# Attention plus two MLPs in split fp32: the probabilities of three batches copied into one-pass tiles before their transposition

## Chip, cores and metric

The kernel runs on one core of one Trainium2 chip. The metric is device time in microseconds of one execution. Five engines work side by side: TensorE (PE, with its weight loads listed as PEld), VectorE (DVE), ScalarE (ACT), GpSimd (POOL) and SyncE (SP), which issues nearly all DMAs.

## What is computed

Four batches of 12 heads, 448 positions, 64 numbers per head; then two MLPs over the 1792 tokens. Inputs of the MLPs arrive as 64-bit floats, everything is computed to fp32 accuracy.

```
q_n, k_n = rmsnorm(q, g_q), rmsnorm(k, g_k)
scores = (q_n @ k_n.T) / sqrt(64);  attn = softmax(scores)
x = (attn @ v)                      # heads joined: 1792 x 768
x = relu(x @ w_in) ** 2 @ w_out     # 768 -> 2048 -> 768
out = ((x @ w1) * (x @ w2)) @ w3 @ w_out2   # 768 -> 1024 -> 768
```

## The kernel before

**Products in three passes.** PE multiplies one-pass fp32 operands (type `F32R`, `fp32r` in the rows). A number is split into a high and a low part of that type, and a product is high·high + high·low + low·high: three matmuls, lines 262 to 264 (`mm3`). `w3 @ w_out2` is multiplied out ahead of time (`gen_w3o`) and stored as `w3o`.

**Weights.** They come in units of 128x384 or 128x512 numbers. In the first MLP pass (batch 0) a unit is loaded as 64-bit words (SP, line 180), its halves are turned into two 32-bit pieces by ACT (line 194) and POOL (line 200), DVE joins them (line 207), and the fp32 unit is stored to DRAM (line 215). The three later batches load that fp32 copy (line 183). Every unit is then split: ACT copies the high part (line 106, `hl<-raw`), POOL or DVE subtracts for the low part (line 114). Four buffers for 64-bit units and four for fp32 ones are used in turn; a load waits for its buffer. `advance` (line 240 onwards) issues loads, pieces, joins and splits a fixed number of units ahead of the matmul that uses them.

**Attention.** The main loop runs over the 48 heads `h` and one more round. Each round has, for head `h`: scores in two halves (`stage_qk`, lines 524 and 525), the maximum on DVE (lines 526, 527), the exponential on ACT (`stage_exp`, line 542), which writes the probabilities `p`, 112 x 448 for each of four chunks. In the same round head `h - 1` is finished: `stage_t` transposes its probabilities on PE, 16 transpositions in four blocks (line 564; three blocks of 128 columns, the last of 64). The probabilities are the stationary operand, so each transposition is a weight load of 128 (or 64) columns and a matmul with the identity `ident`, 112 columns. ACT copies the transposed block as high part (`ptr`, `pte`), DVE subtracts for the low part, and `stage_v` multiplies with `v` (line 616). The normalised keys are transposed too (`stage_k`, line 508): they are split already, lie in `fp32r` tiles and use `ident_r`, an identity of that type.

**Filling.** Between the steps of a round, `fill(n)` puts matmuls of the MLP of the batch before into PE's queue: during heads 0 to 11 the product `w3o`, during heads 12 to 23 the MLP of batch 0 (with the 64-bit weights), during 24 to 35 that of batch 1, during 36 to 47 that of batch 2; that of batch 3 stands alone at the end. Every engine and SP's queue work in order; the order is set by a scheduler when the kernel is built.

**Buffers touched.** `p` has six tiles of 112 x 448 fp32, in pool `t3`; a tile is free again when its head's transpositions are done.

Of the kernel before, what the change touches and what calls it, by code (L numbers as in the profile page):

```python
# [8 lines left out]
F32 = mybir.dt.float32  # L9
F32R = mybir.dt.float32r  # L10
# [19 lines left out]
def attention_moe_kernel(  # L30
# [15 lines left out]
    nc = tc.nc  # L46
    B, P, H, C, D = q_nat.shape
    S = P * C
# [40 lines left out]
    t3 = ctx.enter_context(tc.tile_pool(name="t3", bufs=3))  # L89
# [9 lines left out]
    ident = const.tile([P, P], F32, name="ident")  # L99
    ident_r = const.tile([P, P], F32R, name="ident_r")  # L100
# [3 lines left out]
    def copy_on(eng, out, in_):  # L104
        if eng == "a":
            nc.scalar.activation(out=out, in_=in_, func=AF.Copy)  # L106
        elif eng == "g":
            nc.gpsimd.tensor_scalar(out=out, in0=in_, scalar1=1.0, scalar2=1.0, op0=ALU.mult, op1=ALU.mult)
        else:
            nc.vector.tensor_copy(out=out, in_=in_)  # L110
# [418 lines left out]
    def stage_exp(h, s):  # L529
        if not (0 <= h < NH):  # L530
            return
        d = heads[h]
        nb, o = d.pop("nb"), d.pop("sc")
        i = h % 2
        if s == 0 and i == 0:
            sums2[h // 2] = small.tile([P, 2, C], F32, name="sm", tag="sm")
        sm = sums2[h // 2]
        c0 = 2 * s
        for j in range(2):
            c = c0 + j  # L540
            p = d["p"][c] = t3.tile([P, S], F32, name="p", tag="p", bufs=6)
            nc.scalar.activation(  # L542
                out=p, in_=o[j], func=AF.Exp, scale=d["rq"][:, c:c + 1], bias=nb[:, j:j + 1],
                accum_out=sm[:, i, c:c + 1],
            )
        if s == 1 and i == 1:
            nc.vector.tensor_scalar(out=sm, in0=sm, scalar1=1e-9, scalar2=None, op0=ALU.add)
            rs = small.tile([P, 2, C], F32, name="rs", tag="rs")
            nc.vector.reciprocal(out=rs, in_=sm)
            wide = t1.tile([P, C, 2, D], F32, name="rsw", tag="rsw")  # L550
            nc.gpsimd.tensor_scalar(
                out=wide, in0=rs.rearrange("p i c -> p c i").unsqueeze(3).to_broadcast([P, C, 2, D]),
                scalar1=1.0, scalar2=1.0, op0=ALU.mult, op1=ALU.mult,
            )
            sums2[h // 2] = wide.rearrange("p c i d -> p c (i d)")

    def stage_t(h, kc):
        if not (0 <= h < NH):
            return
        d = heads[h]  # L560
        k0, kn = KCS[kc]
        ps = ps_pt.tile([128, 512], F32, name="pt", tag="pt")
        for c in range(C):
            nc.tensor.transpose(ps[:kn, c * P:(c + 1) * P], d["p"][c][:, k0:k0 + kn], ident)  # L564
        if kn == 128:
            t = t3.tile([128, 2, S], F32R, name="ptr", tag="ptr", bufs=3)
            hi, lo = t[:, 0, :], t[:, 1, :]
            d["pt"][kc] = [hi, lo]
        else:
            t = t1.tile([128, S], F32R, name="pte", tag="pte")  # L570
            hi, lo = t[:kn, :], t[kn:, :]
            d["pt"][kc] = [t]
        copy_on("a", hi, ps[:kn, :S])
        d["lo"].append((lo, ps[:kn, :S], hi.bitcast(F32)))
# [67 lines left out]
    def fill(n):  # L642
# [18 lines left out]
        out=gg, in0=g_sb[:, 0:1], scalar=float(D) ** -0.5, in1=g_sb[:, 1:2], op0=ALU.mult, op1=ALU.mult  # L661
# [8 lines left out]
    for h in range(NH + 1):  # L670
# [5 lines left out]
        stage_qk(h, 0)  # L676
        fill(n)
        stage_exp(h, 0)
        if h % H != 1:
            stage_x(h - 2)  # L680
        stage_t(h - 1, 0)
        stage_t(h - 1, 1)
        fill(n)
        stage_lo(h - 1)
        if h < NH:
            v_prep(h)
        fill(n)
        stage_k(h + 1)
        stage_t(h - 1, 2)
        stage_t(h - 1, 3)  # L690
        fill(n)
        stage_lo(h - 1)
        stage_qk(h, 1)
        fill(n)
        stage_exp(h, 1)
        fill(n)
        stage_v(h - 1)
# [64 lines left out]
```

## Time and profile before

| | us |
|---|---|
| median of 3 runs | 1253.63 (1252.76 to 1253.79) |
| span of the profiled execution, first to last instruction | 1246.1 |
| PE busy | 1173.5 (94%) |
| PE weight loads busy | 1060.8 (85%) |
| POOL, ACT, DVE busy | 780.3, 728.9, 708.0 |
| matmuls / DMA packets | 6192 / 102129 |

The profiled execution is given by its span; its own time is not listed apart, and the three runs lie 6.7 to 7.7 us above the span, for what comes ahead of the first instruction and after the last. A weight load runs beside a matmul, so PE and PEld add up to more than the span. The recorded end of a matmul is modelled; how fast they follow each other is read from their starts.

### The profile page before, as it was taken

How to read it: one execution, taken by the hardware profiler on the slowest of the kernel's cores; microseconds unless marked ns; L12 is line 12 of the kernel's file. 1: busy time of each engine (PE TensorE's matmuls, PEld its weight loads, DVE VectorE, ACT ScalarE, POOL GpSimd, SP SyncE). 2: the span in 40 equal slices, each digit the busy share in tenths (PEclk: the TensorE clock that was granted, in tenths of full speed). 3: DMA queues.
4: the chain of work that ended last, by engine and by line, in shares of the span. 5: the costliest groups of instructions: out<-in, count | busy, mean ns of one | idle time of the engine just before them, and what ended most of it. 6: DMA issues, size and time to landing. Idle time of an engine off the chain costs nothing.

```text
span 1246.1 us, 18719 instructions
## 1 busy us (share of the span) xinstructions
PE 1173.5 (94%) x6192; PEld 1060.8 (85%) x6192; DVE 708.0 (57%) x1314; ACT 728.9 (58%) x1553; POOL 780.3 (63%) x772
## 2 busy tenths in 40 slices
PE   3789999898889899999999999999999999999998
PEld 2678888887777788999999999999999999999998
DVE  6699888867887775547567555655664421012110
ACT  5788876756655655566645555656645554443342
POOL 6775435645675665675776664755766556678773
PEclk9999999899999999999999999999999999999999
DMA  7774446876766655344333344332333333433342
GB/s 218 237 225 137 150 140 183 267 215 217 236 205 212 207 158 159 106 117 113 113 102 114 96 130 128 105 105 85 112 95 88 92 114 107 113 108 108 103 121 94
DMA packets 102129, 178.71 MB, mean 143 GB/s; under 512 B 11056, under 2 KB 65552, under 8 KB 102032
## 3 DMA queue, kind: packets, MB, share of 16 engines
q1 hardware_dynamic: 98576, 172.01, 46.6%
q10 hardware_dynamic: 3456, 5.51, 1.2%
q8 instruction: 49, 0.80, 0.3%
q14 instruction: 48, 0.39, 0.1%
HBM read 149.95 MB, written 27.53 MB: 142 GB/s over the span
## 4 chain that ended last, share of the span: by engine, by line
PE 69%; DVE 10%; DMA 7%; ACT 5%; POOL 5%; issue 4%; SPq 0%; ACTq 0%; DVEq 0%; POOLq 0%
PE mm L263 18%; PE mm L262 18%; PE mm L264 18%; PE pt L564 4%; PE kv L616 4%; POOL hl L114 2%; PE sc L524 2%; DMA raw<-w_in 2%; PE sc L525 2%; DVE raw L207 2%; DVE nb L526 2%; ACT p L542 2%; DMA kn<-k_nat 1%; DMA raw<-w 1%; ACT hl L106 1%
## 5 line engine op out<-in xcount | busy, mean ns | idle before, releaser
L114 POOL TENSOR_TENSOR hl<-raw,hl 128x384 fp32r<-128x384 f32 (+1 forms) x383 | 444.6, 1164 | 254.1 <-ACT hl L106 251.2
L106 ACT ACTIVATE hl<-raw 128x384 fp32r<-128x384 f32 (+1 forms) x416 | 233.2, 564 | 149.2 <-PE mm L264 82.2
L263 PE MATMUL mm<-x,hl 128*128 128x448 f32 (+1 forms) x832 | 306.4, 368 | 9.4 <-POOL x L114 9.4
L262 PE MATMUL mm<-x,hl 128*128 128x448 f32 (+1 forms) x832 | 311.0, 374 | 4.0 <-ACT x L106 1.8
L264 PE MATMUL mm<-x,hl 128*128 128x448 f32 (+1 forms) x832 | 305.5, 367 | 0.9 <-POOL hl L114 0.9
L262 PE MATMUL mm<-act,hl 128*128 128x448 f32 (+1 forms) x640 | 238.6, 373 | 0.0
L263 PE MATMUL mm<-act,hl 128*128 128x448 f32 (+1 forms) x640 | 235.8, 368 | 2.2 <-POOL act L114 1.7
L264 PE MATMUL mm<-act,hl 128*128 128x448 f32 (+1 forms) x640 | 234.7, 367 | 1.4 <-POOL hl L114 1.0
L542 ACT ACTIVATE p<-sc,nb,rr 112x448 f32<-112x448 f32 x192 | 137.3, 719 | 75.4 <-DVE nb L527 74.8
L263 PEld LDWEIGHTS mm<-x,hl 128*128 128x128 f32 x832 | 158.2, 190 | 23.2 <-POOL x L114 11.1
L262 PEld LDWEIGHTS mm<-x,hl 128*128 128x128 f32 x832 | 158.1, 190 | 18.9 <-ACT x L106 2.9
L264 PEld LDWEIGHTS mm<-x,hl 128*128 128x128 f32 x832 | 158.2, 190 | 14.9 <-POOL hl L114 2.0
L200 POOL TENSOR_SCALAR raw<-raw 128x384 uint32<-128x384 uint16 (+1 forms) x110 | 87.7, 798 | 84.6 <-DMA raw<-w_in 35.3
L526 DVE TENSOR_REDUCE nb<-sc 112x1 f32<-112x448 f32 x192 | 113.2, 616 | 37.7 <-PE sc L525 36.7
L263 PEld LDWEIGHTS mm<-act,hl 128*128 128x128 f32 x640 | 122.0, 191 | 12.9 <-POOL act L114 3.0
L264 PEld LDWEIGHTS mm<-act,hl 128*128 128x128 f32 x640 | 122.0, 191 | 11.8 <-POOL hl L114 1.8
L262 PEld LDWEIGHTS mm<-act,hl 128*128 128x128 f32 x640 | 122.2, 191 | 9.4 <-ACT act L106 0.2
L114 DVE TENSOR_TENSOR ptr<-pt,ptr 128x448 fp32r<-128x448 f32 x144 | 86.9, 618 | 69.8 <-ACT ptr L106 69.2
L207 DVE SCALAR_TENSOR_TENSOR raw<-raw 128x384 uint32<-128x384 uint32 (+1 forms) x120 | 85.5, 715 | 51.6 <-POOL hl L114 43.5
L564 PE MATMUL pt<-ident,p 112*128 112x112 f32 (+1 forms) x768 | 99.4, 265 | 12.6 <-DVE ptr L114 9.7
L194 ACT ACTIVATE raw<-raw 128x384 f32<-128x384 f32 (+1 forms) x120 | 71.1, 599 | 68.1 <-DMA raw<-w 25.0
L114 POOL TENSOR_TENSOR act<-gf,act 128x448 fp32r<-128x448 f32 x80 | 96.9, 1212 | 8.1 <-ACT act L106 3.2
(80 smaller groups left out, 1542.7 us busy)
## 6 DMA issues: line engine op xcount, KB each, us to landing
raw<-f_in SPq DMA_DIRECT2D x96, 192.0 KB, 2.4
raw<-f_out SPq DMA_DIRECT2D x72, 256.0 KB, 2.6
raw<-f SPq DMA_DIRECT2D x96, 192.0 KB, 2.4
raw<-w_in SPq DMA_DIRECT2D x32, 384.0 KB, 3.5
raw<-w_out SPq DMA_DIRECT2D x24, 512.0 KB, 4.5
raw<-w SPq DMA_DIRECT2D x32, 384.0 KB, 4.0
raw<-w3o SPq DMA_DIRECT2D x48, 256.0 KB, 2.7
qt<-q_t SPq DMA_DIRECT2D x48, 224.0 KB, 2.8
```

What stands on the lines that cost most here:

```text
L106: nc.scalar.activation(out=out, in_=in_, func=AF.Copy)
L114: e.tensor_tensor(out=out, in0=in0, in1=in1, op=ALU.subtract)
L194: nc.scalar.activation(out=hi, in_=hi, func=AF.Prelu, scale=2.0**-112, alpha=-(2.0**32))
L200: nc.gpsimd.tensor_scalar(out=t[:, :n, 0], in0=low, scalar1=2.0**-13, scalar2=2.0**-14 - 0.5, op0=ALU.mult, op1=ALU.add)
L207: nc.vector.scalar_tensor_tensor(out=f[:, :n].bitcast(U32), in0=t[:, :n, 1], scalar=3, in1=t[:, :n, 0], op0=ALU.logical_shift_left, op1=AL ...
L262: nc.tensor.matmul(ps, w[:, 0, wk, :], x[0], start=(i == 0), stop=False)
L263: nc.tensor.matmul(ps, w[:, 0, wk, :], x[1], start=False, stop=False)
L264: nc.tensor.matmul(ps, w[:, 1, wk, :], x[0], start=False, stop=(i == last))
L526: nc.vector.tensor_reduce(out=nb[:, j:j + 1], in_=o[j], axis=AX.X, op=ALU.max, negate=True)
L542: nc.scalar.activation(out=p, in_=o[j], func=AF.Exp, scale=d["rq"][:, c:c + 1], bias=nb[:, j:j + 1], accum_out=sm[:, i, c:c + 1],)
L564: nc.tensor.transpose(ps[:kn, c * P:(c + 1) * P], d["p"][c][:, k0:k0 + kn], ident)
L616: nc.tensor.matmul(ps[:, :S], w, m, start=(n == 0), stop=(n == len(ops) - 1))
```

## The change

From head 12 on (`h >= H`), the two chunks of probabilities that one `stage_exp` makes are copied by a DMA on SP's queue from `p` to a new tile `pw` of type `F32R`, 112 x 896 words, bit for bit. The transpositions of those heads read `pw` and `ident_r` and write the PSUM tile as `F32R`. `p` becomes three tiles of two chunks each (as many bytes as before); `pw` has three more of that size. The region of SBUF that is kept for DMA descriptors made in software is set to 1 KB.

```
+        pp = t3.tile([P, 2, S], F32, name="p", tag="p")
         for j in range(2):
             c = c0 + j
-            p = d["p"][c] = t3.tile([P, S], F32, name="p", tag="p", bufs=6)
+            p = d["p"][c] = pp[:, j, :]
             nc.scalar.activation(
                 out=p, in_=o[j], func=AF.Exp, scale=d["rq"][:, c:c + 1], bias=nb[:, j:j + 1],
                 accum_out=sm[:, i, c:c + 1],
             )
+        if h >= H:
+            words = t3.tile([P, 2, S], F32R, name="pw", tag="pw")
+            nc.sync.dma_start(out=words.bitcast(F32), in_=pp)
+            d["p"][c0:c0 + 2] = [words[:, 0, :], words[:, 1, :]]
...
         ps = ps_pt.tile([128, 512], F32, name="pt", tag="pt")
+        to, one = (ps.bitcast(F32R), ident_r) if h >= H else (ps, ident)
         for c in range(C):
-            nc.tensor.transpose(ps[:kn, c * P:(c + 1) * P], d["p"][c][:, k0:k0 + kn], ident)
+            nc.tensor.transpose(to[:kn, c * P:(c + 1) * P], d["p"][c][:, k0:k0 + kn], one)
...
-    nc = bacc.Bacc("TRN2", target_bir_lowering=False, num_devices=1)
+    nc = bacc.Bacc("TRN2", target_bir_lowering=False, num_devices=1, dynamic_dma_scratch_size=1024)
```

How the order of the instructions moves, at three places. In the changed kernel the lines behind `stage_exp` have other numbers: the exponential is line 543, the copy 549, the transposition 570.

SP's queue, during the first MLP pass, around the copy of the first half of head 14. Before:

```order
L180 DMA raw_2735<-w_out 128x1024
L215 DMA f_in<-raw 128x384
L180 DMA raw_2783<-w_out 128x1024
L215 DMA f_in<-raw 128x384
L180 DMA raw_2802<-w_out 128x1024
L215 DMA f_out<-raw 128x512
L422 DMA v<-v_in 128x256
```

and now:

```order
L180 DMA raw_2716<-w_out 128x1024
L549 DMA pw<-p 112x896
L215 DMA f_in<-raw 128x384
L180 DMA raw_2764<-w_out 128x1024
L215 DMA f_in<-raw 128x384
L180 DMA raw_2783<-w_out 128x1024
L215 DMA f_out<-raw 128x512
```

The copy stands behind the 51st load of 64-bit weights (`raw_2735` before, `raw_2716` now); the 52nd and 53rd, and three stores, stand behind the copy.

ACT, around the exponentials of the second half of head 14. Before:

```order
L106 ACTIVATE hl<-raw 128x384
L194 ACTIVATE raw_2841<-raw_2841 128x512
L106 ACTIVATE hl<-raw 128x512
L194 ACTIVATE raw_2864<-raw_2864 128x512
L330 ACTIVATE r<-mm 128x448
L106 ACTIVATE hl<-raw 128x512
L333 ACTIVATE act<-r 128x448
L542 ACTIVATE p,sm<-sc,nb,rr 112x448 x2
```

and now:

```order
L106 ACTIVATE hl<-raw 128x384
L194 ACTIVATE raw_2764<-raw_2764 128x512
L106 ACTIVATE hl<-raw 128x512
L194 ACTIVATE raw_2783<-raw_2783 128x512
L330 ACTIVATE r<-mm 128x448
L106 ACTIVATE hl<-raw 128x512
L333 ACTIVATE act<-r 128x448
L543 ACTIVATE p,sm<-sc,nb,rr 112x448 x2
```

The rows read alike, but the weight units are others: ahead of these exponentials stood the units loaded 54th and 55th (`raw_2841`, `raw_2864`), now stand those loaded 52nd and 53rd (`raw_2764`, `raw_2783`). The turning of the 64-bit weights has moved back by two units against the attention there.

PE, at the first two blocks of transpositions of a head of batch 1. Before:

```order
L263 MATMUL mm<-x,hl 128x448
L264 MATMUL mm<-x,hl 128x448
L564 MATMUL pt<-ident,p 128x112 x8
L262 MATMUL mm<-x,hl 128x448
L263 MATMUL mm<-x,hl 128x448
```

and now:

```order
L263 MATMUL mm<-x,hl 128x448
L264 MATMUL mm<-x,hl 128x448
L570 MATMUL pt<-ident_r,pw 128x112 x8
L262 MATMUL mm<-x,hl 128x448
L263 MATMUL mm<-x,hl 128x448
```

PE's order stays as it was but for two exchanges of neighbours; the transpositions stand at the same place and read `pw`.

## Rows read from the trace of the kernel before

**Rows 1.** Windows: stretch, length, busy time of PE, PEld, DVE, ACT, POOL, clock, DMA.

```profile
192.00:498.00 306.00, 276.57 (x1416) 243.16 (x1415) 231.33 (x415) 191.69 (x414) 183.07 (x195) 0.97 0.68 206
498.00:768.00 270.00, 270.00 (x1466) 247.87 (x1465) 161.21 (x285) 156.21 (x341) 178.18 (x166) 1.00 0.39 113
768.00:1028.00 260.00, 260.00 (x1411) 238.62 (x1410) 134.08 (x244) 147.58 (x323) 162.11 (x148) 1.00 0.34 100
```

**Rows 2.** Waits of PE, 192 to 498 us: waited for, total us, times, longest.

```profile
PE sc L524 <- ACT p L542: 14.9, 13, 2.7
PE pt L564 <- DVE ptr L114: 9.2, 10, 3.4
```

**Rows 3.** Timeline of PE, 619.6 to 621.3 us: start, length, what (head 29).

```profile
620.07 0.93 PE L564 MATMUL pt<-ident,p 112*128 112x112 f32 x8
...
621.06 0.36 PE L263 MATMUL mm<-act,hl 128*128 128x448 f32 x1
621.26 0.37 PE L264 MATMUL mm<-act,hl 128*128 128x448 f32 x1
```

**Rows 4.** Timeline of PE, 114.8 to 116 us, a run of key transpositions.

```profile
115.00 0.34 PE L264 MATMUL mm<-x,hl 128*128 128x384 f32 x1
115.17 0.46 PE L508 MATMUL kv<-ident_r,khl 112*128 112x112 f32 x4
...
115.71 0.34 PE L263 MATMUL mm<-x,hl 128*128 128x384 f32 x1
```

**Rows 5.** Timeline of PEld near 626.5 us, in narrow windows.

```profile
626.43 0.23 PEld L508 LDWEIGHTS kv<-ident_r,khl 112*128 112x128 f32 x2
...
626.69 0.20 PEld L564 LDWEIGHTS pt<-ident,p 112*128 112x128 f32 x2
```

**Rows 6.** Groups by form, PEld, whole span: count, busy us, mean ns, idle.

```profile
L564 PEld LDWEIGHTS pt<-ident,p 112*128 112x128 f32 x576 | 63.0, 143 | 17.8 <-DVE ptr L114 9.9 <-issue 3.0 <-PE kv L508 0.3
...
L564 PEld LDWEIGHTS pt<-ident,p 112*64 112x64 f32 x192 | 19.1, 113 | 3.2 <-DVE ptr L114 2.0 <-PE pt L564 0.4
```

**Rows 7.** DMA issues, 192 to 498 us: count, KB each, median us to landing.

```profile
raw<-w SPq DMA_DIRECT2D x32, 384.0 KB, 4.0
...
kn<-k_nat SPq DMA_DIRECT2D x3, 448.0 KB, 4.2
```

**Rows 8.** DMA, 498 to 768 us: queue (packets, MB, share), one issue.

```profile
q1 hardware_dynamic: 18614, 28.80, 37.2%
...
kn<-k_nat SPq DMA_DIRECT2D x3, 448.0 KB, 3.8
```

**Rows 9.** Timelines of ACT and PE: last exponential and first transposition, heads 12, 18, 32.

```profile
192.08 0.19 ACT L542 ACTIVATION_READ_ACCUMULATOR p<-sc,nb,rr 112x1 f32 x1
...
194.58 0.93 PE L564 MATMUL pt<-ident,p 112*128 112x112 f32 x8
...
339.96 0.20 ACT L542 ACTIVATION_READ_ACCUMULATOR p<-sc,nb,rr 112x1 f32 x1
...
345.45 0.93 PE L564 MATMUL pt<-ident,p 112*128 112x112 f32 x8
...
681.53 0.19 ACT L542 ACTIVATION_READ_ACCUMULATOR p<-sc,nb,rr 112x1 f32 x1
...
687.20 0.93 PE L564 MATMUL pt<-ident,p 112*128 112x112 f32 x8
```

**Rows 10.** Waits of SP's queue, 498 to 768 us.

```profile
SPq L183 <- POOL hl L114: 190.8, 100, 5.3
```

**Rows 11.** Timelines near 220 us: SP's queue, and the first half of head 14.

```profile
218.20 0.33 SPq L180 DMA_DIRECT2D raw<-w_out  x1
...
222.78 0.20 ACT L542 ACTIVATION_READ_ACCUMULATOR p<-sc,nb,rr 112x1 f32 x1
```

**Rows 12.** Chain of waits, 192 to 498 us, shares of the stretch by line.

```profile
by line: issue 10.0%; POOL hl L114 8.9%; DMA raw<-w_in 7.5%; DVE raw L207 6.1%; DMA raw<-w 5.3%; ACT p L542 4.6%; DVE nb L526 4.2%; PE mm L262 3.6%; PE mm L264 3.5%; PE mm L263 3.4%; DMA raw<-w_out 3.1%; ACT hl L106 3.0%; DMA kn<-k_nat 2.9%
```

## Prediction

> **What bounds the kernel now.** I read the busy times by stretch first, then PE's waits, then single stretches of the timelines. The change touches heads 12 to 47, which fill three stretches: 192 to 498 us (heads 12 to 23, beside the first MLP pass with its 64-bit weights), 498 to 768 and 768 to 1028. In the second and third PE is busy for 270.0 of 270 and 260.0 of 260 us [rows 1]: PE alone sets their length, and a nanosecond taken from it is a nanosecond of the end. In the first it is busy for 276.6 of 306 us, so 29.4 us are idle, and the largest items are waits for the exponential on ACT (14.9 us, 13 times) and for the low parts of transposed blocks on DVE (9.2 us, 10 times) [rows 2]. There the chain of waits runs through the weights: DMA of w_in, w and w_out 7.5, 5.3 and 3.1%, POOL's splits 8.9%, DVE's joins 6.1% [rows 12]. So the change has a clear place to win in the last two stretches, and a stretch with no room to spare ahead of them.
>
> **What a transposition costs.** Eight fp32 transpositions start at 620.07; the second matmul behind them starts at 621.06, and the next 0.20 later [rows 3]. 0.99 less an ordinary 0.20 to 0.21 us leaves 785 ns, 98 ns for each. The new kind stands in the trace already, in the transpositions of keys: a one-pass fp32 tile of 112 partitions and 128 columns as weights, 112 columns of identity moving. A run of four of these starts at 115.17, the second matmul behind it at 115.71; less an ordinary 0.17, that is 0.37 us, 92 ns each [rows 4]. A longer run goes at the pace of its weight loads: from the second load of the four at 626.43 to the load behind the fourth at 626.69 there are three steps, 87 ns each [rows 5]. So the new kind isn't four times as fast, nor twice: the matmul gets shorter, and the weight load becomes the limit. For blocks of 128 columns I take 98 - 87 = 11 ns at most and 98 - 92 = 6 at least, 9 as the middle. For the blocks of 64 columns no one-pass row exists. A load of 64 columns takes 113 ns where one of 128 takes 143 [rows 6], so 30 less; 87 - 30 = 57 ns, and the gain is 98 - 57 = 41. Bounds are 6 ns (a load that costs as much as one of 128) and 98 - 50 = 48 (112 moving columns at the granted 2.4 GHz are 47 ns, and something for the start). A head has 12 of the one and 4 of the other: 12 x 9 + 4 x 41 = 272 ns, between 96 (16 x 6) and 324 (12 x 11 + 4 x 48). If loads of the new kind could follow as fast as the fp32 pair in the same group, whose second starts 61 ns after the first (0.20 - 0.14 from 626.69), it would be 16 x 37 = 592 ns; I take the keys' rows, which are of the same type and shape, and keep 592 for the far end.
>
> The Trainium skill (TensorE: Matmul & The Clock Gate, LDWEIGHTS) says that a weight load takes its columns divided by 1.2 GHz, which would be 107 ns for 128 columns and 53 for 64. By that rule the 128-column transpositions would get slower, and a head would gain only 12 x (98 - 107) + 4 x (98 - 53) = 72 ns. The trace has 87 and 61 ns where the rule has 107, so it speaks against the rule's size.
>
> In the last two stretches 24 heads gain 24 x 0.272 = **6.5 us**, all of it on PE. In the first stretch 12 heads gain 3.3 us of PE time; with a tenth of that stretch not PE's, and the waits beside it not shortened, I count half, **1.6 us**.
>
> **What the copies cost.** 72 copies of 112 x 896 words are added, 401 KB each (392 in the rows' KB). Size and partitions are nearest to the loads of k, 448 KB over 112 partitions: 4.2 us from issue to landing in the first stretch, weights of 384 KB take 4.0 there [rows 7], and 3.8 us in the second [rows 8]. Between SBUF and SBUF no row exists. I take 4.2 and 3.8, and 3.2 to 5.2 as bounds. Up to one other issue (0.33 us) [rows 11] stands ahead of a copy that is ready, so some 4.5 and 4.1 us from the last exponential to the transpositions. What time is there? For head 12 the last exponential ends at 192.27 and its transpositions start at 194.58: 2.3 us. For head 18 it is 340.16 to 345.45: 5.3 us [rows 9]. These are the least and the most of the twelve heads of the first stretch, which spread between them. Spread evenly, the mean shortfall against 4.5 is (4.5 - 2.3)² / (2 x 3.0) = 0.81 us, 9.7 us over 12 heads. PE would wait in a new place, but each such wait also lets ACT and DVE catch up, and the 24.1 us of waits of [rows 2] shrink by some of it. Between nothing and all I take half: **4.8 us**. With 3.2 + 0.3 it is half of 2.9 (1.4 us), with 5.2 + 0.3 all of 20 us.
>
> From head 24 on the least time between is that of head 32, 681.72 to 687.20, 5.5 us [rows 9]. 4.1 is under it. There SP waits 1.9 us at a time for a buffer (190.8 us in 100 waits, 5.3 the longest) [rows 10], and a copy can stand behind such a wait. What is left for head 32, 1.4 us, covers most of one; I count nothing, and name it below.
>
> The Trainium skill (DMA: Bandwidth & Descriptors, Anatomy of one DMA) gives a fixed 2.0 us plus bytes at 436 GB/s, which would be 2.9 us for a copy. By that the first stretch would lose 0.8 us in place of 4.8, and the sum would be 1246.3. The loads of k take 4.2 us here against 3.1 by the rule, so the trace disagrees.
>
> The rest costs nothing: the copies' traffic lies beside PE, DMA being busy for 0.39 and 0.34 of the later stretches [rows 1]; ACT and the three pairs of `p` keep their size; `p` comes free earlier, when copied; no DMA is issued by POOL, so the 1 KB is room alone.
>
> **The sum.** -6.5 - 1.6 + 4.8 = -3.3 us. The trace's span is 1246.1 us and the median of the runs 1253.6, 7.5 more for what lies around it, which the change doesn't touch. **1250.3 us** against 1253.6.
>
> **The rivals.**
>
> *Copies hold the weights up (slower).* SP's queue works in order, and a copy waits in it for its exponential. In the trace the 52nd load of 64-bit weights went out at 218.20, while the first half of head 14 was done at 222.98 [rows 11]; in the new order that load stands behind the copy, 4.8 us later. Behind it in the DMA rings it also waits for the copy's bytes: the queue needs 0.372 x 270 us for 28.8 MB [rows 8], so 1.4 us for 0.401 MB. For it: the first stretch's chain runs through weight loads, 15.9% of 306 us or 49 us, a dozen loads of 4 us [rows 12]. Against it: ACT's order has moved back by one or two weight units at those places, as the loads do. If half of the dozen are set back by 1.4 us, 8.4 us come on top: 1258.7; if all, and some of the wait with it, 1267. It decides once more than 3.3 us (two or three loads) are lost so.
>
> *Nothing gained at the loads (no change).* At the low bound, 24 x 0.096 = 2.3 us and 0.6 in the first stretch, less 4.8: 1255.5. For it: 92 ns in the one run of keys that is followed by plain matmuls [rows 4]. It is then slower by 0.15%. The rule of the Trainium skill on weight loads (above) belongs here: 72 ns a head, 1.7 + 0.4 - 4.8, 1256.3.
>
> *Loads at the fp32 pace.* 592 ns a head: -14.2 - 3.6 + 4.8, 1240.6. Against it stand the keys' rows of the same type.
>
> *Copies late in the last two stretches too.* One of 5.2 us behind a wait of 1.9 comes 1.6 us after head 32's 5.5; with 24 heads at half of that, 19 us more, 1269. For most heads there is more time than for head 32.
>
> *The type changes nothing.* If a transposition of the new type took 98 ns, only the waits would be left: 1253.6 + 4.8 = 1258.4. The keys' loads speak against it.
>
> **How the numbers follow.** 0.2% (2.5 us) is about what a measurement of this kernel can tell from no change. The forecast has 0.38 (own range 1246.5 to 1253, of which 0.05 within 0.2%); weights held up 0.27 (0.22 slower, 0.05 within); nothing gained 0.20 (0.16 within, 0.04 slower); loads at the fp32 pace 0.08; late copies 0.04; no effect of the type 0.03. Faster: 0.33 + 0.08 = 0.41; within: 0.05 + 0.05 + 0.16 = 0.26; slower: 0.22 + 0.04 + 0.04 + 0.03 = 0.33. The range 1241 to 1262 takes in the forecast with its bounds, nothing gained, and the milder part of weights held up; the far ends of the others are left out.
>
> **What would show it.** Transpositions of heads 12 on should follow at some 87 ns, those of 64 columns at 50 to 60; the stretch from head 24 to 47 should be 6 to 7 us shorter with PE still busy all through. Copies should land 3.5 to 4.5 us after their issue. In the first stretch PE should wait for `pw` by a few us in all, heads 12 and 13 first, and its waits for ACT's exponential should shrink. I am wrong if ACT or POOL wait much longer for weights there than now, if PE waits for `pw` after head 24, or if the blocks of 64 columns are no faster than the others.

## The result, and the profile after

The changed kernel takes **1239.49 us** (1239.34 to 1240.05, 4 runs) against 1253.2 us (1251.29 to 1253.79, 4 runs): ratio 0.9894, 95% interval 0.9878 to 0.9909. The forecast was 1250.3 with a range from 1241 to 1262, so the sign was right and the size was not: 13.7 us were gained, not 3.3. That the sign came out right is luck, as the fifth run below shows.

First the windows of the changed kernel, columns as in [rows 1].

```profile
192.00:498.00 306.00, 278.95 (x1451) 248.61 (x1450) 236.37 (x416) 193.84 (x419) 191.13 (x198) 0.97 0.77 243
498.00:768.00 270.00, 267.64 (x1461) 244.16 (x1460) 160.57 (x288) 156.19 (x340) 178.03 (x166) 1.00 0.51 148
768.00:1028.00 260.00, 260.00 (x1419) 237.60 (x1418) 134.20 (x244) 146.99 (x321) 163.98 (x148) 1.00 0.45 134
```

In the first stretch PE has 35 more matmuls done in the same 306 us than in [rows 1]; in the second it is idle for 2.4 us where it had no idle time. DMA is busier by 0.09 to 0.12, which is the copies (without them, in the sixth run below, DMA is at 0.69, 0.38 and 0.33). How long each part lasts is read from the first transposition of heads 12, 24, 36 and 47 in PE's timeline:

```profile
194.23 0.37 PE L570 MATMUL pt<-ident_r,pw 112*128 112x112 f32 x3
...
501.66 0.54 PE L570 MATMUL pt<-ident_r,pw 112*128 112x112 f32 x5
...
770.25 0.53 PE L570 MATMUL pt<-ident_r,pw 112*128 112x112 f32 x5
...
1012.41 0.37 PE L570 MATMUL pt<-ident_r,pw 112*128 112x112 f32 x3
```

In the trace of before that of head 12 stands at 194.58 [rows 9], and the others here:

```profile
508.79 0.45 PE L564 MATMUL pt<-ident,p 112*128 112x112 f32 x3
...
776.46 0.55 PE L564 MATMUL pt<-ident,p 112*128 112x112 f32 x4
...
1020.69 0.55 PE L564 MATMUL pt<-ident,p 112*128 112x112 f32 x4
```

So heads 12 to 23 went from 314.2 to 307.4 us, heads 24 to 35 from 267.7 to 268.6, heads 36 to 46 from 244.2 to 242.2. The gain lies where the forecast expected a loss, and of the 6.5 us that it expected behind head 24 only 1.1 are left (0.9 more and 2.0 less). The spans differ by 8.3 us (1246.1 and 1237.8), the medians by 13.7, because the profiled execution of before was a quick one: in all later runs the time is 1.7 to 2.3 us above the span, so it took some 1248. The 7.5 us that the forecast took for what lies around the span were 2 us of that and a quick execution; they stand on both sides of its sum and change nothing in the 3.3. Runs of before lay between 1246.1 and 1257.0 in the study.

PE's waits from 192 to 498 us, to be held against [rows 2]:

```profile
PE pt L570 <- DMA pw<-p: 11.1, 7, 2.6
PE sc L524 <- ACT p L543: 5.7, 5, 2.1
...
PE pt L570 <- DVE ptr L114: 1.9, 3, 1.0
```

There is a new wait, for the copies, of 11.1 us. But the two waits of [rows 2] fell from 24.1 to 7.6 us, by more than the new one adds. What made them shrink is the question of the experiments. The DMA issues of the same stretch, and of the twelfth run below, which has this order and no copies:

```profile
raw<-w_out SPq DMA_DIRECT2D x24, 512.0 KB, 6.2
raw<-w SPq DMA_DIRECT2D x32, 384.0 KB, 4.9
pw<-p SPq DMA_DIRECT2D x25, 392.0 KB, 4.4
...
kn<-k_nat SPq DMA_DIRECT2D x3, 448.0 KB, 5.3
```

```profile
raw<-w_out SPq DMA_DIRECT2D x24, 512.0 KB, 5.3
raw<-w SPq DMA_DIRECT2D x32, 384.0 KB, 3.9
```

A load of w lands after 4.9 us where it took 4.0, one of k after 5.3 where it took 4.2 [rows 7], one of w_out after 6.2 where it took 4.5. The copies' share is the difference to the twelfth run: 1.0 us for w, 0.9 for w_out; the rest of w_out's came with the order. The copies land 4.4 us after their issue, as forecast.

### The profile page after: what moved, and what is told of

It is laid out like the page before. It is cut to its first block, busy times and chain, and to the rows that moved or that the text cites. A ratio compares the mean times of both kernels' runs of the same rounds, so it can differ in the third digit from the quotient of the medians.

```text
span 1237.8 us, 18914 instructions
## 1 busy us (share of the span) xinstructions
PE 1166.3 (94%) x6192; PEld 1054.4 (85%) x6192; DVE 710.7 (57%) x1314; ACT 727.7 (59%) x1553; POOL 784.9 (63%) x772
## 4 chain that ended last, share of the span: by engine, by line
PE 59%; DMA 4%; DVE 4%; ACT 2%; POOL 1%; issue 1%; ACTq 0%; SPq 0%; POOLq 0%; DVEq 0%
PE mm L262 17%; PE mm L264 17%; PE mm L263 17%; PE kv L622 3%; PE pt L570 2%; DMA pw<-p 2%; PE sc L525 1%; PE sc L524 1%; DMA raw<-w 1%; POOL hl L114 1%; ACT p L543 1%; DMA kn<-k_nat 1%; PE kv L508 1%; DVE nb L526 1%; DVE raw L207 0%
## 5 line engine op out<-in xcount | busy, mean ns | idle before, releaser
L200 POOL TENSOR_SCALAR raw<-raw 128x384 uint32<-128x384 uint16 (+1 forms) x110 | 86.3, 785 | 73.3 <-DMA raw<-w_in 25.8
L334 DVE TENSOR_TENSOR gf<-mm,r 128x448 f32<-128x448 f32 x64 | 39.8, 622 | 97.7 <-ACT r L330 97.3
```

The lines of the kernel that those rows point to most:

```text
L200: nc.gpsimd.tensor_scalar(out=t[:, :n, 0], in0=low, scalar1=2.0**-13, scalar2=2.0**-14 - 0.5, op0=ALU.mult, op1=ALU.add)
L334: nc.vector.tensor_tensor(out=gf, in0=ps, in1=r, op=ALU.mult)
```

## The experiments

All are compared with the kernel before on the same chip. "Heads 12 to 23" is the time from the first transposition of head 12 to that of head 24 in the profiled execution: 314.2 us before, 307.4 in the changed kernel. It is one execution of each. How far such a time can stray shows ahead of what any run changes: the first transposition of head 11 starts between 177.1 and 181.6 us in the twenty traces. So a few us in heads 12 to 23 decide nothing by themselves, and where they matter the medians are given too, each as its difference to the runs of before beside it. Behind head 24 the stretches repeat to 0.1 or 0.2 us wherever the kernel is the same there.

### 1 to 4: one part of the change at a time

The first has the small scratch alone.

```
-    nc = bacc.Bacc("TRN2", target_bir_lowering=False, num_devices=1)
+    nc = bacc.Bacc("TRN2", target_bir_lowering=False, num_devices=1, dynamic_dma_scratch_size=1024)
```

> The kernel before with the 1 KB scratch alone; the order of the instructions is the same on every engine. Two theories on the 13.7 us: the profiled span fell by 8.3 us (1246.1 to 1237.8) and the median by 13.7, so either 5 us come from what lies around the span, which only the scratch could change, or the profiled execution of before was a quick one and its span stands for 1247.8. Scratch matters: 1248 us, time less span 1.7 where it was 7. Scratch does nothing: 1251 to 1254 us, ratio 0.998 to 1.002, time less span 1.7 and a span of 1249 to 1252.

Measured: 1250.85 us, ratio 0.9998 (0.9982 to 1.0014); heads 12 to 23 314.2. The scratch is worth nothing by itself, and the time lies 2.1 to 2.3 us above the span with it as without.

The second has the change with fp32 copies and fp32 transpositions (some expectations call these two-pass; no trace counts passes).

```
-            words = t3.tile([P, 2, S], F32R, name="pw", tag="pw")
+            words = t3.tile([P, 2, S], F32, name="pw", tag="pw")
...
-        to, one = (ps.bitcast(F32R), ident_r) if h >= H else (ps, ident)
+        to, one = ps, ident
```

> Copies as in the change, but into fp32 tiles that are transposed as before: the copies without the cheaper transpositions. If the gain is that of the transpositions, this is slower than before: the waits for the copies stay (13 us in the changed kernel's trace, most of them in 192 to 498 us), 1253 to 1262 us. If the gain in 192 to 498 us comes from the other order of loads and conversions and from what the waits let catch up, that stretch keeps its 7 us and only the last two stretches lose: 1243 to 1247 us.

Measured: 1252.63 us, ratio 1.000 (0.9986 to 1.0014); heads 12 to 23 317.6, between the two ranges. It looked as if copies cost nothing. But the scheduler had given this kernel a third order in the first stretch, neither that of before nor that of the changed kernel, so the run mixes two things.

The third and fourth have the change from head 24 on, and for heads 12 to 23 alone.

```
-        if h >= H:
+        if h >= 2 * H:
```

> Copies and one-pass transpositions from head 24 on alone. By the changed kernel's trace heads 24 to 47 took 510.8 us where they had taken 511.9: if that is all they bring, 1250 to 1252 us. If the loads' pace that I forecast (0.27 us a head) holds there, 1246 to 1248. In both, heads 12 to 23 take 313 to 315 us as before.

```
-        if h >= H:
+        if H <= h < 2 * H:
```

> Copies and one-pass transpositions for heads 12 to 23 alone. If the 6.9 us of this stretch come from the change there, 1244 to 1247 us, with 306 to 309 us between the first transpositions of heads 12 and 24. If they were chance of that execution, 1250 to 1254 us and 311 to 316.

Measured: from head 24 on 1249.31 us, ratio 0.9977 (0.9960 to 0.9994); for heads 12 to 23 alone 1240.81 us, ratio 0.9907 (0.9884 to 0.9929), that stretch at 305.4 us. The third lies between its two ranges, the fourth below its first one. So most of the gain, 11.5 of 13.7 us, is in heads 12 to 23, where the third kernel has before's order on ACT, DVE and POOL and the fourth the changed kernel's.

### 5 to 8: the order held, the parts changed

To part the order from the work, a kernel's instructions are chained on each engine, each behind the one that stands ahead of it in a list taken from another kernel. No work is added, and the chain itself costs nothing where that can be seen: in the tenth, thirteenth and fourteenth run, chained in before's order from head 24 on, those stretches take 267.8 and 244.2 us, and in before 267.7 and 244.2. (The lines are written short; the lists hold every instruction.)

```
         attention_moe_kernel(tc, *args)
+        every = [x for blk in tc._region_blocks() for x in blk.instructions]
+        for engine, places in ORDER.items():
+            for a, b in zip(places, places[1:]):
+                tc.add_manual_dep(every[b], every[a].name, no_sync, reason="order")
```

> The whole change (copies, one-pass transpositions from head 12 on, small scratch), but with the instructions of TensorE, ScalarE, VectorE, GpSimd and SyncE held in the order in which the kernel before has them; only the 72 copies are new among SyncE's. It asks whether the about 11.6 us that the change gains in heads 12 to 23 come from the order that the scheduler now chooses there or from the cheaper transpositions themselves. Theory A (the new order of ScalarE, VectorE, GpSimd and SyncE in the first stretch carries it): without that order the first stretch stays near 314 us from the first transposition of head 12 to that of head 24, and only the later stretches gain, about 3 us: near 1249.5 us, ratio near 0.998. Theory B (the transpositions in one-pass type carry it, because the scores' PSUM and the stage behind them come free sooner): the first stretch is near 306 us and the time near 1240 us, ratio near 0.990.

Measured: **1267.24 us**, ratio 1.012 (1.0094 to 1.0146); heads 12 to 23 329.9.

> The kernel before, with no copies and its two-pass transpositions, but with its instructions held in the order in which the changed kernel has them on TensorE, ScalarE, VectorE, GpSimd and SyncE. Theory A (order): the first stretch gains nearly all that the change gains there, so heads 12 to 23 take near 306 us and the time is near 1243 us, ratio near 0.992. Theory B (type): the order is worth nothing by itself, near 1252.5 us, ratio 1.000 within 0.002, heads 12 to 23 near 314 us.

Measured: **1235.26 us** (1232.31 to 1239.01), ratio 0.9875 (0.9848 to 0.9901); heads 12 to 23 299.8. Without a copy and without a one-pass transposition of probabilities it gains all that the changed kernel gains (0.9894, 0.9878 to 0.9909), and by its median 4 us more.

> Copies into plain fp32 tiles and two-pass transpositions, as in the second run, but with the order of the changed kernel on all five engines, so that it differs from the changed kernel in the type of the transpositions alone. Theory A (order): near the changed kernel less its direct gains of 2.4 us in the first stretch and 3 us in the others, so near 1245 us, ratio near 0.994, heads 12 to 23 near 309 us. Theory B (type): like the second run, near 1252.6 us, ratio near 1.000, heads 12 to 23 near 316 us.

Measured: 1243.78 us, ratio 0.9931 (0.9915 to 0.9948); heads 12 to 23 307.9.

The eighth has no copies; the exponential writes the one-pass tiles.

```
-        pp = t3.tile([P, 2, S], F32, name="p", tag="p")
+        pp = t3.tile([P, 2, S], F32R if h >= H else F32, name="p", tag="p")
...
-            nc.sync.dma_start(out=words.bitcast(F32), in_=pp)
```

> No copies: from head 12 on the exponential itself writes tiles of the one-pass type, which rounds the probabilities to that type (so the low parts that are multiplied later hold nothing), and the transpositions are one-pass; all engines keep the order of the kernel before. It prices the cheap transpositions without copies and without a new order. Theory A (order): 36 heads by 0.2 us, some 7 us at most and less where loads end the waits in the first stretch: 1246 to 1249 us, heads 12 to 23 at 311 to 314 us. Theory B (type): heads 12 to 23 near 305 us and the time 1236 to 1241 us.

Measured: 1246.81 us, ratio 0.9955 (0.9934 to 0.9976); heads 12 to 23 317.3, 24 to 35 265.2, 36 to 46 241.8, so all of its gain lies behind head 24. It rounds the probabilities, so it is a probe and no replacement.

Theory B misses in all four. Theory A has the times of the seventh and eighth (the eighth's stretch of 317.3 us lies above its 311 to 314), but was too mild for the others: it had put the order at the 11.6 us of the fourth run, and the fifth came out 18 us slower and the sixth 8 us faster than it said, since the order is worth more and the copies cost more than their sum had shown. With the twelfth run (below) heads 12 to 23 make a table, in us:

| work | order of before | order of the changed kernel |
|---|---|---|
| as before | 314.2 | 299.8 |
| copies, fp32 transpositions | not run | 307.9 |
| one-pass transpositions, no copies | 317.3 | 301.9 |
| both (the change) | 329.9 | 307.4 |

Read across, the order takes 14 to 22 us off; by the medians of whole runs it is 17 without the change's work and 29 with it. Read down, the cheaper transpositions show no gain clear of that spread in this stretch (one-pass against fp32: +3.1, +2.1, and -0.5 with copies; by the medians, less what is gained behind head 24, -0.3, -0.3 and -2.7). The copies add 8.1 us with fp32 transpositions and 5.5 with one-pass ones in the new order (by the medians, again without what lies behind head 24, 7.0 and 4.5), 12.6 in the old one (16.8). PE's rows from 192 to 498 us say the same, first the windows row of the fifth run and its waits, then of the sixth:

```profile
192.00:498.00 306.00, 266.87 (x1318) 231.91 (x1319) 224.65 (x397) 182.33 (x393) 171.00 (x185) 0.93 0.75 228
```

```profile
PE pt L570 <- DMA pw<-p: 13.3, 7, 3.3
PE sc L524 <- ACT p L543: 12.4, 10, 2.8
PE pt L570 <- DVE ptr L114: 4.5, 6, 1.8
```

```profile
192.00:498.00 306.00, 286.61 (x1493) 253.59 (x1492) 241.49 (x423) 197.17 (x429) 194.98 (x202) 0.98 0.69 212
```

```profile
PE sc L524 <- ACT p L542: 6.0, 6, 2.4
PE pt L564 <- DVE ptr L114: 4.0, 6, 1.6
```

The sixth has 24.1 us of waits of [rows 2] down to 10.0 by order alone. In the fifth the waits for the exponential stay at 12.4 and those for the copies come on top. PE is idle for 39 us in the one and for 19 in the other, and its granted clock is 0.93 in the one and 0.98 in the other: of the 30 us between them some 20 are idle time, and the rest goes beside the lower clock.

What a copy does to the load behind it, in the fifth run: SP's queue near 217 us, and the load from the chain of waits.

```profile
216.03 0.52 SPq L549 DMA_DIRECT2D pw<-p  x1
217.07 0.34 SPq L414 DMA_DIRECT2D qt<-q_t  x1
217.57 1.18 SPq L180 DMA_DIRECT2D raw<-w_out  x1
```

```profile
217.57 7.49 DMA raw<-w_out
```

That load, the 50th of the 64-bit weights, lands 7.5 us after its issue; the same one took 6.9 in the trace of before and 5.8 in the eighth run, which has the same order and no copies. In all, ACT's and POOL's conversions wait 133.7 us for loads in this stretch, in the eighth run 113.9, and SP's queue stands for 36.9 us at copies that wait for ACT.

### 9 and 12: the terms put together

The ninth: copies and one-pass transpositions from head 24 on, as in the third, in the changed kernel's order.

> Copies and one-pass transpositions for heads 24 to 47 alone, as in the third run, with all engines in the order of the changed kernel. If the order, the copies and the type are terms that add, it takes the sixth run's 1235.3 us less the about 3 us that the third run gained in heads 24 to 47: near 1232.3 us, heads 12 to 23 near 300 us, and it beats both kernels. If the copies of later heads disturb more than they did in the third run, or the order is only worth its 14 us with nothing else on the queue, it is at 1235 us or above.

Measured: 1234.70 us (1233.90 to 1236.16), ratio 0.9867 (0.9843 to 0.9892); heads 12 to 23 301.8, 24 to 35 269.2, 36 to 46 241.8. It beats the kernel before, and the changed kernel by 5 us of the median, though the two intervals still overlap; it doesn't beat the sixth: the 2.4 us of heads 36 to 46 are there, heads 24 to 35 lose 1.5 us, and PE has 2.2 us of idle time in them. The expected 1232.3 was missed.

> No copies: the exponential writes the one-pass type from head 12 on (the probabilities are rounded to it), transpositions one-pass, the order that of the changed kernel. If cheap transpositions gain their 0.2 us a head where nothing waits and little in heads 12 to 23, it is the sixth run's 1235.3 us less 24 x 0.2 and less 0 to 2.4 us: 1228 to 1231 us. If the first stretch gets nothing from them, as in the eighth run, 1231 us with heads 12 to 23 near 300 us. If the copies were what the order was worth its gain for, above 1235 us.

Its edit is that of the eighth, its list that of the changed kernel. Measured: 1231.36 us, ratio 0.9841 (0.9817 to 0.9864); heads 12 to 23 301.9, 24 to 35 265.7, 36 to 46 241.8. So without copies the one-pass transpositions are worth 2.1 and 2.4 us in the later stretches, and nothing that can be seen in the first.

### 10, 11, 13, 14: is it the conversions that wait for loads?

In the new order 51 of the 78 conversions of 64-bit weights on ACT (line 194) stand later among ACT's instructions, by 2.5 places on the mean of all, and 50 of their low halves on POOL (line 200), by 1.2. Exponentials stood behind conversions, and conversions wait for loads; so I took that for the cause (theory C; E with both engines' halves). The tenth and eleventh move ACT's conversions of heads 12 to 23 two places in before's order, the thirteenth moves both halves, the fourteenth POOL's alone. The edits are written short.

```
+ORDER = order_of_before
+ORDER["Activation"] = moved(ORDER["Activation"], conversions, 2)
```

> The kernel before in its own order on every engine but ScalarE: there each of the 78 conversions of 64-bit weights that lie in heads 12 to 23 stands two instructions later, which puts 12 of them behind an exponential that they stood ahead of (the changed kernel's order puts 18 behind). Theory C (what the new order is worth comes from conversions no longer holding up exponentials and copies out of PSUM while they wait for their loads): part of the 14 us, so 1243 to 1250 us, the waits of ScalarE's conversions for loads in 192 to 498 us below the 49 us of before, heads 12 to 23 at 306 to 312 us. Theory D (the order on VectorE and GpSimd carries it, where the joins and subtractions stand): 1252 us within 2, or slower, since the joins on VectorE now wait for later conversions.

Measured: 1250.31 us, ratio 0.9981 (0.9964 to 0.9998); heads 12 to 23 316.6 in the profiled execution. A little faster at best, though ACT's conversions wait 8.6 us for loads where they waited 48.9: theory C fails.

> The same with each of the 78 conversions two instructions sooner on ScalarE, which puts 11 of them ahead of an exponential that they stood behind. Theory C: the waits for loads grow and the exponentials come later, 1255 to 1262 us, heads 12 to 23 at 317 to 323 us. Theory D: 1252 us within 2.

Measured: **1330.59 us**, ratio 1.063 (1.0602 to 1.0657); heads 12 to 23 395.2, far beyond what theory C had expected. PE's waits for ACT show why: the conversions now hold the high parts of the weights up as well as the exponentials.

```profile
PE sc L524 <- ACT p L542: 20.4, 11, 4.4
PE mm L262 <- ACT hl L106: 20.3, 8, 4.7
```

```
+ORDER["Activation"] = moved(ORDER["Activation"], conversions, 2)
+ORDER["Pool"] = moved(ORDER["Pool"], low_halves, 1)
```

> The kernel before in its own order, except that in heads 12 to 23 the 78 conversions of 64-bit weights stand two instructions later on ScalarE and their low halves one instruction later on GpSimd (in the changed kernel's order they stand on average 2.5 and 1.2 places later). Theory E (both engines' halves wait for the same load with attention's work queued behind, and one alone moves the wait to the other): the waits for loads on ScalarE and GpSimd in 192 to 498 us fall together from some 98 to 55 us or less, VectorE's waits at the joins below 35 us, heads 12 to 23 near 304 us and the time 1238 to 1245 us. Theory F (the gain comes from the rest of the order, such as the subtractions and joins that trade places with attention's work one by one): 1249 to 1255 us.

Measured: 1248.75 us, ratio 0.9955 (0.9937 to 0.9973); heads 12 to 23 314.0 in the profiled execution, which was the slowest of four (1252.79).

> GpSimd's low halves alone one instruction later, ScalarE as before. If GpSimd's wait by itself held up the joins: 1240 to 1247 us. Theory E: a smaller part, 1247 to 1252 us. Theory F: 1252 us within 2 or slower.

Measured: 1254.61 us, ratio 1.0017 (1.0005 to 1.0028); heads 12 to 23 320.2: no gain.

The thirteenth is the telling one. Before, ACT's conversions wait for loads for 48.9 us in 192 to 498 us and POOL's halves for 48.8:

```profile
ACT raw L194 <- DMA raw<-w: 25.0, 15, 3.5
ACT raw L194 <- DMA raw<-w_out: 12.3, 9, 2.8
ACT raw L194 <- DMA raw<-w_in: 11.6, 8, 2.5
...
POOL raw L200 <- DMA raw<-w_in: 23.0, 10, 4.8
POOL raw L200 <- DMA raw<-w: 16.0, 16, 2.0
POOL raw L200 <- DMA raw<-w_out: 9.8, 8, 2.7
```

in the thirteenth for 13.2 and 2.9:

```profile
ACT raw L194 <- DMA raw<-w: 5.2, 4, 2.1
ACT raw L194 <- DMA raw<-w_in: 4.6, 4, 1.4
ACT raw L194 <- DMA raw<-w_out: 3.4, 4, 1.9
...
POOL raw L200 <- DMA raw<-w: 2.6, 5, 1.1
POOL raw L200 <- DMA raw<-w_in: 0.3, 1, 0.3
```

Some 82 of 98 us of waits are gone and the kernel is 4.7 us faster by the medians. In the sixth they only fell to 32.0 and 26.1, and it is 17 us faster. So theory E falls as the whole cause: a large wait in the view is not what it is worth. SP's own waits in the stretch show what the thirteenth left as it was, the loads' wait for the joins that free their buffers. Before, in the thirteenth, in the sixth:

```profile
SPq L180 <- DVE raw L207: 139.9, 65, 5.4
```

```profile
SPq L180 <- DVE raw L207: 140.0, 63, 5.9
```

```profile
SPq L180 <- DVE raw L207: 108.0, 51, 4.6
```

The joins themselves wait 42.9, 40.1 and 25.8 us on DVE. The conversions stood later and found their loads landed, but the joins came no sooner, nor the next loads.

### 16 to 18: the rest of the order without the conversions

The changed kernel's order on before's work, as in the sixth, but the conversions back among the others where before has them: on both engines, on ACT alone, on POOL alone.

```
+ORDER = order_of_changed
+ORDER["Activation"] = with_places_of(order_of_before, conversions)
+ORDER["Pool"] = with_places_of(order_of_before, low_halves)
```

> The kernel before in the changed kernel's order, but in heads 12 to 23 the 78 conversions of 64-bit weights on ScalarE and their low halves on GpSimd stand among the other instructions of their engines where the kernel before has them. Theory G (the rest of the order carries it, VectorE's above all, since moving the conversions brought 5 us at most): 1235 to 1241 us, heads 12 to 23 at 300 to 306 us. Theory H (the conversions' places carry it, but only where VectorE's joins fit them, which the tenth and thirteenth runs did not have): 1248 us or more, heads 12 to 23 above 311 us.

> The same with ScalarE's conversions alone put back, GpSimd's low halves where the changed kernel has them. Theory G: 1235 to 1240 us. Theory H: 1244 us or more.

> The same with GpSimd's low halves alone put back, ScalarE's conversions where the changed kernel has them. Theory G: 1235 to 1240 us. Theory H: 1238 us or more, less than the seventeenth.

Measured: 1274.79 us, ratio 1.0175 (1.0147 to 1.0202), heads 12 to 23 337.0; 1259.64, 1.0061 (1.0043 to 1.0079), 320.9; 1258.25, 1.0056 (1.0037 to 1.0075), 324.3. All three are slower than before, so theory G falls, and H stands: the conversions' places are needed, and since moving them by themselves (tenth, thirteenth) gained 5 us at most, they need those of the other instructions too. In the sixteenth POOL's waits for loads are the largest seen:

```profile
POOL raw L200 <- DMA raw<-w_in: 32.3, 12, 8.7
POOL raw L200 <- DMA raw<-w_out: 30.7, 11, 9.4
POOL raw L200 <- DMA raw<-w: 16.4, 15, 2.3
```

My reading, which no run shows by itself: loads, both halves of a conversion and the join go round through four buffers, and a half that stands too early on its engine waits there for a load that still waits for a join, with all that is queued behind it. The new order without the conversions' places loses 24 us, with them it gains 17; exactly those places in before's order were not run, the thirteenth comes nearest to it. Which exchanges of two instructions matter most was not found, and ACT's, DVE's or POOL's new order by itself was not tried.

### 15: the lowest median that keeps fp32 probabilities

```
-        if h >= H:
+        if h >= 3 * H:
```

> The order of the changed kernel, with copies and one-pass transpositions for heads 36 to 47 alone, where no wait for a copy was seen. The sixth run's 1235.3 us less the 2.4 us that the third and ninth runs gained from head 36 on: 1232.9 us, with heads 24 to 35 at 267.8 us and heads 36 to 46 at 241.8. If the runs of this order differ by over 2 us among themselves in heads 12 to 23, it can't be told from the sixth run.

Measured: 1233.40 us (1231.45 to 1236.71), ratio 0.9840 (0.9817 to 0.9862); heads 24 to 35 267.7, 36 to 46 241.8, both as expected, and heads 12 to 23 301.0. It beats both kernels, and its own intervals overlap with those of the sixth and ninth, so which of the three is best stays open.

## Why the prediction was wrong, step by step

**The pace of transpositions: right.** Eight of them, and then four of 128 and four of 64 columns, in the changed kernel's timeline of PE:

```profile
613.13 0.80 PE L570 MATMUL pt<-ident_r,pw 112*128 112x112 f32 x8
613.76 0.44 PE L262 MATMUL mm<-act,hl 128*128 128x448 f32 x1
614.04 0.36 PE L263 MATMUL mm<-act,hl 128*128 128x448 f32 x1
...
619.60 0.73 PE L570 MATMUL pt<-ident_r,pw 112*128 112x112 f32 x8
620.17 0.44 PE L262 MATMUL mm<-act,hl 128*128 128x448 f32 x1
620.46 0.36 PE L263 MATMUL mm<-act,hl 128*128 128x448 f32 x1
```

By the forecast's own count (to the second matmul behind, less 0.20 us) eight take 0.71 us, 88 ns each, between the forecast's 87 and 89. The mixed eight take 0.86 us to that matmul; before they took 1.02:

```profile
626.72 0.96 PE L564 MATMUL pt<-ident,p 112*128 112x112 f32 x8
...
627.74 0.37 PE L263 MATMUL mm<-act,hl 128*128 128x448 f32 x1
```

So a head gains 0.08 + 0.16 = 0.24 us, forecast 0.272 (by the twelfth run's stretches, 4.5 us over 23 heads, 0.2). From start to start the blocks of 64 columns go at 54 to 59 ns, forecast 57; but the last fp32 transposition of a block let the next matmul start 28 ns later, the last one-pass one only after some 55 (64 columns) or 86 ns (128), and that takes some back.

The Trainium skill (TensorE: Matmul & The Clock Gate, LDWEIGHTS) has a load take its columns divided by 1.2 GHz, 107 and 53 ns. The trace agrees for 64 columns (54 to 59 ns from start to start) and not for 128 (86 to 88).

**6.5 us in the later stretches: too much by a third.** In the twelfth run, without copies, they are 2.1 + 2.4 = 4.5 us, over 23 of the 24 heads. In the changed kernel's trace 1.1 of these are left. Waits for copies in heads 27, 31 and 35 take 2.4 back; where the other 1.0 went isn't known. I had counted nothing there, with 1.4 us of room for head 32, and had named a wait for `pw` behind head 24 as a sign of being wrong: it came, at other heads than I looked at. The view of the tile `pw` (first its DMA issues, in ns, then why PE and PEld were idle ahead of transpositions, then the time to landing) has copies as late as 6.8 us:

```profile
L549 SPq DMA_DIRECT2D pw<-p x72: 517/517/599, 185.4 to 1006.0; - x72
...
  DMA pw<-p: 28.7, 21
...
DMA to landing us min/median/max: 3.2/4.2/6.8
```

**1.6 us in the first stretch from cheaper transpositions: not seen,** by the table above, and too small to be told from its spread.

**4.8 us lost to copies in the first stretch: 12.6 in the order that the forecast reckoned with.** That is before's order (fifth against eighth run); in the changed kernel's it is 5.5 to 8.1, by the medians 4.5 to 7.0, so that the size came near in an order that I hadn't priced. The landing (4.4 us) and PE's new wait were right, in heads 12, 14, 15, 17, 20, 21 and 22, though not in 13. The forecast let half of the new waits be made good by shorter old ones, and in the fifth run that is about so: 13.3 us of new ones, and the old ones of [rows 2] down from 24.1 to 16.9. What it left out is the weights' side: with the order held, the copies made a load of w, w_in or w_out longer by 1.0, 1.2 and 0.9 us (changed kernel against twelfth run), which I had kept for a rival.

The Trainium skill (DMA: Bandwidth & Descriptors, Anatomy of one DMA) gives its figure for DMAs that GpSimd issues; SP issues these. An estimate by it is 2.9 us for a copy; the trace has 4.2 in the median, beside other traffic, so the measurement decides here.

**The step that failed: the sum has no term for the order.** The forecast said what had moved (conversions "back by one or two weight units") and used it only as an argument against the rival *copies hold the weights up*; it put the move itself at nothing. The scheduler's new order is worth 22 us of heads 12 to 23 on the same work (329.9 to 307.4), 14 without copies. Held to before's order, as in the fifth run, the change loses 15 us and stands at 1267.24 us. That is the far price of the rival (1267), but the rival counted delayed loads alone, and in the run 13.3 us are PE's own waits for copies; what the delayed loads cost by themselves isn't parted, so the equal number is luck.

From before to the changed kernel in steps: order -16.8 us (sixth), copies in that order +8.5 (seventh less sixth), type -5.4 (changed less seventh, each against the runs of before beside it). They add up to the 13.7 because each step starts where the last ended; taken in another sequence the terms are others, since copies cost more in the old order. The rival *loads at the fp32 pace* was near the time (1240.6) for a reason that the trace refutes.

## What to carry to other kernels

When a scheduler orders the program, an edit that changes an instruction's type or adds one may change the order of everything near it, and in a stretch where no engine is full that can outweigh the edit: hold the order and change the work, then hold the work and change the order. Do not price a reordering by the waits in a view; here removing 82 of 98 us of one kind brought 4.7 us, and moving conversions two places the other way cost 78. Look for the gain of an order where PE is not full; a cheaper instruction on PE pays where PE is full, here if its copies have time to land (heads 36 to 47).

## What was unexpected in the hardware

- A copy from SBUF to SBUF of 392 KB takes 517 ns of SP's queue to issue, where a load of weights takes 330 [rows 11], and lands about as late (4.2 us) as loads of its size from DRAM.
- 25 runs of before spread over 11 us. Four of the changed kernel lie within 0.7 and four of the twelfth within 1.2, but four of the sixth, in the same order, spread over 6.7, so a small spread isn't shown to belong to the order.
- In the 306 us of the first stretch the granted clock (a mean of times at 2.4 and at 1.2 GHz, as a share of 2.4) was 0.98 with 19.4 us of PE idle (sixth run), 0.97 with 29.4 (before) and 0.93 with 39.1 (fifth). In these three a wait goes with a loss beyond its own length. But in the fourteenth it was 0.98 with 36.9, so the sum of idle time doesn't set it.
